# Wide tiles: input transposed by the DMA engines, and two outputs in seven block products

## The chip, the core and the metric

The kernel runs on one core of one Trainium2 chip. The core has five engines that run their own instruction streams and wait for each other through semaphores: TensorE (PE in the profile; its weight loads are PEld) for matrix products into PSUM, VectorE (DVE) and ScalarE (ACT) for elementwise work, GpSimd (POOL) for elementwise work and for issuing loads, and SyncE (SP), which issues the output's stores. Times are microseconds of the device for one execution; each kernel is run several times and the median is given.

## The reference

Eight batches of eight heads, 576 tokens, 64 elements a head: attention in a causal window of 64 tokens. Its result, 4608 tokens by 512, goes through a gated feed-forward layer of width 1536.

```python
def _attn_ref(q, k, v):
    B, H, S, D = q.shape
    window = 64
    scale = 1.0 / np.sqrt(D)
    scores = scale * np.matmul(q, k.transpose(0, 1, 3, 2))
    pos = np.arange(S)
    rel = pos[:, None] - pos[None, :]
    mask = (rel >= 0) & (rel < window)
    scores = np.where(mask, scores, -1000000000.0)
    scores = scores - np.max(scores, axis=-1, keepdims=True)
    attn = np.exp(scores)
    attn = attn / (np.sum(attn, axis=-1, keepdims=True) + 1e-09)
    return np.matmul(attn, v).astype(np.float32)

def _moe_ref(x, w_gate, w_val, w_out):
    gate = np.maximum(x @ w_gate, 0.0)
    val = x @ w_val
    return (gate * val @ w_out).astype(np.float32)
```

Inputs and output are 32-bit floats in HBM; the kernel multiplies in 16-bit floats and sums in 32.

## The kernel before

The 4608 tokens are cut into ten tiles: tiles 0 to 3 of 384 tokens and the wide tiles 4 to 9 of 512 (`starts`, `widths`, lines 70 to 76). The text counts them from 0, so the eighth and ninth tile are 7 and 8, and `LAST` is 9. Only the wide tiles matter here.

**Attention of a wide tile.** Queries are handled in quads of four windows of 64 (`q_st`, `scores`): TensorE makes the scores of four head pairs in four PSUM banks (line 253), ScalarE takes the exponential into `pw` (line 389), VectorE masks it (line 394). `values(t, hh)` then makes the product with v for one half of the heads (`t_pv`, line 422) into three banks, with the sum of the weights as a 65th column; VectorE takes the reciprocal (`t_recip`, line 436), multiplies (`t_norm`, line 441) into the tile `xw`, and transposes in blocks of 32x32 (`t_turn`, line 447) into `xt`, where channels lie on partitions. Before the change the rows of a result are channel groups: 32 tokens of each of four heads lie on the 128 partitions.

**Hidden stage (`fast_hidden`).** The gate is a plain product (line 582) that ScalarE passes through a relu into `r` (line 586). The product with `w_val` uses Strassen's scheme in Winograd's form: seven block products P1 to P7 (line 573) in place of eight. It needs four differences of the input's blocks (`x_form`, tile `xc`, line 459, on VectorE) and four of the weight's blocks (`w_form`, tile `vs`, line 480, on GpSimd). Partial sums are combined on the way: bank A collects P1, P6, P7, P4; ScalarE copies it out between them (`snap`, line 593), VectorE adds such a copy to bank B or C (`add`, tile `vsum`, line 600), and GpSimd multiplies by the relu into `g_sb` (line 606); one quarter is multiplied by VectorE straight from PSUM (`direct`, line 613). P3 goes into bank C after the sum with "u3" has been read from it. This is done in three groups of four chunks of 128 hidden channels. A pair such as (1,1) names the half of the hidden channels and the half of the tokens of a product in `g_sb`.

**Output stage (`fast_output`).** For each of four blocks of 128 tokens, 12 products of 512 columns with `wo` (line 658) go into one bank; ScalarE copies it (line 663) into one of three `o_sb` buffers and SP stores it (line 665). Ahead of the four blocks stand, for the tiles to come, the two halves of `values(t + 1)` and two `scores(t + 2)` (list `between`). The last block of tile 9 is cut in three (`output_last`, line 703).

**What sets the order.** Nothing reorders instructions on the chip. The `Weaver` (lines 20 to 43) writes the order out when the kernel is built: it keeps a planned clock, which the issue of a product moves on, and a heap of callbacks with due times; `W.advance` issues what is due. `bank()` and the loops on `done` issue callbacks ahead of time where a product needs their result or a bank. Each engine then runs its stream in this order, and an instruction that waits holds up what stands behind it on its engine. GpSimd's stream has also the loads of q, k (line 173) and v (line 199), the copies that spread v over partitions (lines 208, 210), and SP's stream the stores. A tile pool gives each tile name some buffers (`bufs`); a new use waits for the old one's readers.

`zero` and `zero32` (lines 732 to 735) are tiles of zeros for a few products early on that keep TensorE busy.

Of the kernel before, what the change touches and what calls it, by code (L numbers as in the profile page):

```python
# [10 lines left out]
FP32 = mybir.dt.float32  # L11
# [35 lines left out]
def kernel(  # L47
# [25 lines left out]
    NL = (NT - NS * TT) // WT  # L73
    assert NT == NS * TT + NL * WT and TT % 128 == 0
# [20 lines left out]
    vs = persist.tile([128, 4, 2, 128 * HF], FP16)  # L95
    qTs = [persist.tile([128, 2, S, 2], FP16, name=f"qT{i}") for i in range(2)]
# [307 lines left out]
    def t_pv(t, hh, banks, give):  # L404

        if t not in wides:
            wides[t] = {"pv": {}, "give": give, "x": a_n.tile([128, 2, WS, 2, D // 2], FP16, name="xw", bufs=1),
                        "r": a_n.tile([128, 2, WS, 1], FP32, name="rw")}
        d = wides[t]
        d["pv"][hh] = banks  # L410
        unread.update(map(id, banks))
        for qh in range(2):
            qd = 2 * (t - NS) + qh
            while quads[qd].get("masked", 0) < G:
                W.pop()
            for i in range(QW):
                b, vw = divmod(q_window(qd, i), NG)
                for s in range(2):
                    n = 2 * (QW * qh + i) + s
                    to = banks[n // BS][:, VW * (n % BS):]  # L420
                    for j in range(G):
                        nc.tensor.matmul(to[32 * j:32 * j + 32, 0:D + 1],  # L422
                                         quads[qd]["p"][j][:, QW * hh + i, 32 * s:32 * s + 32],
                                         v16s[b % 2][:, vw, G * hh + j, 0:D + 1],
                                         start=True, stop=True, skip_group_check=True)

    def t_part(d, hh, k):

        s0, s1 = BS * k, min(BS * k + BS, WS)
        return d["pv"][hh][k][:, 0:(s1 - s0) * VW].rearrange("p (s c) -> p s c", c=VW), s0, s1  # L430

    def t_recip(t, hh):
        d = wides[t]
        for k in (2, 0, 1):
            pv, s0, s1 = t_part(d, hh, k)
            nc.vector.reciprocal(d["r"][:, hh, s0:s1], pv[:, :, D:D + 1])

    def t_norm(t, hh, k):
        d = wides[t]
        pv, s0, s1 = t_part(d, hh, k)  # L440
        nc.vector.tensor_tensor(d["x"][:, hh, s0:s1], pv[:, :, 0:D].rearrange("p s (c e) -> p s e c", e=2),
                                d["r"][:, hh, s0:s1, :, None].to_broadcast([128, s1 - s0, 2, D // 2]), MUL)
        read(d["pv"][hh][k], d["give"])

    def t_turn(t, hh):
        dst = xt_tile(t)[:, 2 * hh:2 * hh + 2].rearrange("p e (s c) -> p s e c", c=32)
        nc.vector.transpose(dst, wides[t]["x"][:, hh])
# [4 lines left out]
    def x_form(t, n):  # L452
# [3 lines left out]
        xt, xc = xt_tile(t), xcs[t]  # L456
        b11, b12, b21, b22 = (xt[:, 2 * k:2 * k + 2, HT * h:HT * h + HT] for k in range(2) for h in range(2))
# [5 lines left out]
    def values(t, hh, T, banks=None):  # L463
# [7 lines left out]
        for n in ((0,), (1, 2, 3))[hh]:  # L471
            W.at(T + 4.0 + 0.4 * n, lambda n=n: x_form(t, n))

    def w_form(n, j):
# [5 lines left out]
        nc.gpsimd.tensor_tensor(vs[:, n, :, c], x, y, op)  # L480

# [65 lines left out]
    def fast_hidden(t):  # L547

        g_sb, done = gs[t] = g_sb_p.tile([128, NF, WT], FP16, name="g_sb"), {}
        xt, xc = xt_tile(t), xcs[t]  # L550
        b11, b12, b21, b22 = (xt[:, 2 * k:2 * k + 2, HT * h:HT * h + HT] for k in range(2) for h in range(2))
# [3 lines left out]
        def group(j):  # L555
# [21 lines left out]
            def gate(n):  # L577
# [3 lines left out]
                for k in range(NC):  # L581
                    nc.tensor.matmul(to, wg[:, k, 128 * ff:128 * ff + 128], xt[:, k], start=(k == 0), stop=(k == NC - 1))  # L582
                W.clock += 4 * (WT + 7) / 2400.0

                def relu():
                    nc.scalar.activation(r4[:, n], to, ACT.Relu)  # L586
                    free.append(to)
# [8 lines left out]
            def add(delay, to, name, last, n, h):  # L596

                def summed():
# [5 lines left out]

                    def mult():
                        nc.gpsimd.tensor_tensor(gh[:, 2 * j + HF * n:2 * j + HF * n + 2, h], rh[:, 2 * n:2 * n + 2, h], pair(v), MUL)  # L606
                        done[2 * j + HF * n, h] = done[2 * j + HF * n + 1, h] = True
                    W.at(max(W.clock, at["relus", n]) + 0.7, mult)
# [30 lines left out]
            add(0.1, "C", "u2", True, 0, 1)  # L639

        for j in range(NF // 4):
            group(j)

    F_LAST = [f for j in range(NF // 4) for f in (2 * j + HF, 2 * j + HF + 1, 2 * j, 2 * j + 1)]

    def fast_output(t, between):

        g_sb, done = gs[t]
        for sub, before in enumerate(between):
# [11 lines left out]
            def evac(op=op, sub=sub):  # L661
# [3 lines left out]
                nc.sync.dma_start(out[bass.ds(starts[t] + sub * 128, 128)], o_sb)  # L665
            W.at(W.clock, evac)

# [28 lines left out]
    def output_last(t):  # L696
# [3 lines left out]
        for c0, c1, queue in ((0, 256, nc.sync), (256, 384, nc.sync), (384, DM, nc.scalar)):  # L700
# [4 lines left out]
            o_sb = consts.tile([128, c1 - c0], FP32, name=f"o_last{c0}")  # L705
            nc.scalar.copy(o_sb, op[:, 0:c1 - c0])
            queue.dma_start(out[bass.ds(starts[t] + last * 128, 128), c0:c1], o_sb)
# [11 lines left out]
    with tc.manual_schedule():  # L719
# [12 lines left out]
        zero = consts.tile([128, 512], FP16)  # L732
        nc.vector.memset(zero, 0.0)
        zero32 = consts.tile([128, 384], FP32)
# [89 lines left out]
        for u in (4, 5):  # L824
            W.at(52.0, lambda u=u: v_spread(u, pool))
        pair(2, 55.5, 58.5, 61.9)
# [22 lines left out]
        LAST = NS + NL - 1  # L849
        SLOTS = (2.6, 6.53 + 0.8, 6.53 + 2.6, 2 * 6.53 + 0.8)  # L850

        def ahead(t):
# [9 lines left out]
            if t == NS - 1:  # L862
                qk_ahead(NS + 1, T + 11.5, (0.0, 1.4, 8.0, 9.4))
                for qd, x in ((0, 6.0), (1, 9.2), (2, 22.6), (3, 25.8)):
# [34 lines left out]
        for t in range(NS, NS + NL):  # L899
# [10 lines left out]
            if t == LAST:  # L910
                fast_output(t, between[:-1])
                W.drain()
                output_last(t)
            else:
# [32 lines left out]
```

## Time and profile before

| | |
|---|---|
| time, median of 3 runs | 321.8 us (321.8 to 322.2) |
| the profiled execution: its time, its span | 322.06 us, 320.2 us |
| granted clock of TensorE | 0.995 |
| start of the wide tiles' hidden stages, 4 to 9 | 122.3, 157.2, 190.2, 223.1, 256.0, 287.4 us |
| last product | 317.4 us |

The span is the stretch between the first and the last instruction that the profile shows; the rest of the time lies around it. Busy shares are averages over stages, so the stages are looked at one by one: a window gives the busy time of each engine between two times, the timeline gives instructions in order, and the chain of waits goes back from the last instruction to what released each step.

### The profile page before, as it was taken

The numbers are of one execution on the slowest core, as the hardware profiler recorded it, in microseconds if no ns is written. First come the engines' busy times: TensorE is split into PE (matmuls) and PEld (weight loads), VectorE is DVE, ScalarE is ACT, GpSimd is POOL, SyncE is SP. The second block draws the span as 40 slices with busy tenths as digits, with TensorE's granted clock in tenths as the row PEclk, the third lists the DMA queues.
The fourth block names the chain that finished last, engine by engine and source line by source line (L and its number), as shares of the span: only waits on it lengthen the run. The fifth ranks groups of instructions, "written<-read, shape, count | busy, mean of one in ns | idle before, by whom it ended". The sixth has DMA issues, their size and how long they took to land.

```text
span 320.2 us, 9481 instructions
## 1 busy us (share of the span) xinstructions
PE 308.8 (96%) x4077; PEld 190.1 (59%) x4077; DVE 203.2 (63%) x397; ACT 158.1 (49%) x310; POOL 177.8 (56%) x206
## 2 busy tenths in 40 slices
PE   4799999999899999999999999999999999999996
PEld 2586958655546555665566556655665566546654
DVE  6937962667993996779576857686337734643420
ACT  3644325533524616752765276627652666326632
POOL 8859336215988506799168925980495036404540
PEclk9889999999999999999999999999999999999999
DMA  8999998946299149806910691039001100020002
GB/s 218 183 196 205 194 120 161 171 98 99 30 174 165 21 90 160 57 1 104 219 36 0 97 220 43 2 50 127 35 0 34 69 34 3 2 98 35 0 33 102
DMA packets 52491, 29.52 MB, mean 92 GB/s; under 512 B 38880, under 2 KB 43872, under 8 KB 52448
## 3 DMA queue, kind: packets, MB, share of 16 engines
q0 software_dynamic: 46688, 18.29, 49.3%
q1 hardware_dynamic: 5616, 10.55, 9.3%
q8 instruction: 32, 0.52, 0.7%
q14 instruction: 11, 0.09, 0.1%
q10 hardware_dynamic: 144, 0.07, 0.1%
HBM read 37.75 MB, written 9.44 MB: 147 GB/s over the span
## 4 chain that ended last, share of the span: by engine, by line
PE 89%; DVE 3%; ACT 2%; POOL 2%; DMA 2%; issue 1%; DVEq 0%; POOLq 0%
PE bank L658 19%; PE bank L582 19%; PE bank L538 17%; PE bank L573 17%; PE bank L673 10%; PE bank L253 3%; PE bank L422 2%; DVE p L292 2%; DMA v<-in_v_dram 2%; ACT pw L389 1%; PE bank L311 1%; DVE g_sb L525 1%; PE bank L703 1%; POOL v L199 1%; DVE qT L193 0%
## 5 line engine op out<-in xcount | busy, mean ns | idle before, releaser
L606 POOL TENSOR_TENSOR g_sb<-r,vsum 128x512 f16<-128x512 f32 x54 | 68.1, 1276 | 77.7 <-DVE vsum L600 75.7
L600 DVE TENSOR_TENSOR vsum<-bank,snap 128x512 f32<-128x512 f32 x54 | 37.3, 691 | 60.1 <-PE bank L573 36.5
L582 PE MATMUL bank<-xt,wg 128*128 128x512 f16 x288 | 73.9, 379 | 0.0
L658 PE MATMUL bank<-wo,g_sb 128*128 128x512 f16 x276 | 62.9, 380 | 0.0
L586 ACT ACTIVATE r<-bank 128x512 f32<-128x512 f32 x72 | 43.2, 600 | 32.3 <-PE bank L582 32.3
L658 PEld LDWEIGHTS <-g_sb 128*128 128x128 f16 x276 | 25.5, 98 | 28.9
L582 PEld LDWEIGHTS <-wg 128*128 128x128 f16 x288 | 28.2, 98 | 18.6
L525 DVE TENSOR_TENSOR g_sb<-r,bank 128x384 f16<-128x384 f32 x48 | 25.9, 550 | 20.3 <-PE bank L538 18.8
L522 ACT ACTIVATE r<-bank 128x384 f32<-128x384 f32 x48 | 23.7, 496 | 29.4 <-PE bank L538 20.3
L573 PEld LDWEIGHTS <-vs 128*128 128x128 f16 x288 | 28.0, 98 | 15.6 <-issue 1.6
L538 PE MATMUL bank<-xt,wg 128*128 128x192 f16 (+1 forms) x256 | 36.5, 296 | 0.5 <-DVE g_sb L525 0.4
L663 ACT COPY o_sb<-bank 128x512 f32<-128x512 f32 x23 | 13.5, 586 | 45.2 <-PE bank L658 43.2
L593 ACT COPY snap<-bank 128x512 f32<-128x512 f32 x54 | 31.6, 586 | 8.4 <-PE bank L573 8.4
L199 POOL DMA_DIRECT2D v<-in_v_dram x41 | 34.7, 865 | 1.8 <-DMA q<-in_q_dram 1.0
L538 PE MATMUL bank<-xt,wv 128*128 128x192 f16 (+1 forms) x256 | 34.3, 286 | 0.0
L673 PE MATMUL bank<-wo,g_sb 128*128 128x512 f16 x144 | 32.8, 379 | 0.2 <-DVE g_sb L525 0.2
L538 PEld LDWEIGHTS <-wg 128*128 128x128 f16 x256 | 24.3, 102 | 9.8 <-issue 0.9
L573 PE MATMUL bank<-xc,vs 128*128 128x256 f16 x216 | 29.4, 272 | 0.4 <-ACT snap L593 0.4
L208 POOL COPY v<-v 64x512 f16<-64x512 f16 (+1 forms) x22 | 16.1, 732 | 23.7 <-DMA v<-in_v_dram 22.6
L538 PEld LDWEIGHTS <-wv 128*128 128x128 f16 x256 | 22.9, 98 | 8.1
L394 DVE TENSOR_TENSOR pw<-pw,mask 128x512 f16<-128x512 f16 x48 | 20.2, 437 | 11.2 <-ACT pw L389 10.5
L389 ACT ACTIVATE pw<-bank 128x512 f16<-128x512 f32 x48 | 25.9, 608 | 1.5 <-PE bank L253 1.0
(69 smaller groups left out, 358.6 us busy)
## 6 DMA issues: line engine op xcount, KB each, us to landing
out_dram<-o_sb SPq DMA_DIRECT2D x35, 256.0 KB, 3.0
k<-in_k_dram POOLq DMA_DIRECT2D x15, 288.0 KB, 5.3
q<-in_q_dram POOLq DMA_DIRECT2D x15, 288.0 KB, 7.3
v<-in_v_dram POOLq DMA_DIRECT2D x31, 128.0 KB, 8.0
wg<-in_moe_w_gate_dram POOLq DMA_DIRECT2D x6, 256.0 KB, 6.4
wv<-in_moe_w_val_dram POOLq DMA_DIRECT2D x6, 256.0 KB, 8.2
wo<-in_moe_w_out_dram POOLq DMA_DIRECT2D x3, 512.0 KB, 11.9
v<-in_v_dram POOLq DMA_DIRECT2D x10, 64.0 KB, 5.9
```

The costliest lines, as they stand in the source:

```text
L199: nc.gpsimd.dma_start(v16s[b % 2][lo:hi, g, :, 0:64], v[b, :, 64 * g - 64 + lo:64 * g - 64 + hi].rearrange("h p d -> p h d"))
L389: nc.scalar.activation(d["p"][g].rearrange("p n c -> p (n c)"), d["st"][g], ACT.Exp, scale=scale)
L525: nc.vector.tensor_tensor(g_sb[:, f:f + w, c0:c0 + n], part(r_sb), part(h2), MUL)
L538: nc.tensor.matmul(h[:, b * n:b * n + n], wt[:, c, (f + b) * 128:(f + b) * 128 + 128], xt[:, c, c0:c0 + n], start=(c == 0), stop=(c == NC ...
L573: nc.tensor.matmul(at[to][:, HT * i:HT * i + HT], w[:, k, 128 * i:128 * i + 128], x[:, k], start=(first and i == 0 and k == 0), stop=(k == ...
L582: nc.tensor.matmul(to, wg[:, k, 128 * ff:128 * ff + 128], xt[:, k], start=(k == 0), stop=(k == NC - 1))
L586: nc.scalar.activation(r4[:, n], to, ACT.Relu)
L593: nc.scalar.copy(at[name], at["A"])
L600: nc.vector.tensor_tensor(v, at[to], at[name], ADD)
L606: nc.gpsimd.tensor_tensor(gh[:, 2 * j + HF * n:2 * j + HF * n + 2, h], rh[:, 2 * n:2 * n + 2, h], pair(v), MUL)
L658: nc.tensor.matmul(op, g_sb[:, f, 128 * sub:128 * sub + 128], wo[:, f], start=(i == 0), stop=(i == NF - 1))
L673: nc.tensor.matmul(op, g_sb[:, f, bass.ds(sub * 128, 128)], wo[:, f], start=(f == 0), stop=(f == NF - 1))
```

## The change

It has four parts.

- `t_pv` takes halves of the tokens (quads) in place of halves of the heads, and puts 128 tokens on the partitions, even ones ahead of odd ones. `t_norm` writes `xw` so that a row is a token. `t_turn` is now a DMA that transposes, issued by SP, in place of the VectorE transpose. The order of tokens within `xt` changes, so the views in `x_form`, `fast_hidden` and the stores (`rows_of`) change with it: the two halves of the tokens are the even and the odd ones. All four `x_form` stand behind the second half, 2 us later on the planned clock than before.
- `wo_form`: twelve differences of `wo`'s blocks on GpSimd into a new tile `ws`; six are planned at 50.5 and later, six in tile 3.
- For tiles 7 and 8 `g_form` makes twelve differences of `g_sb`'s blocks on VectorE into `s_sb`, and `block_output` makes the output by seven block products in place of eight, with three copies by ScalarE into `snap`, three sums by VectorE and one copy by ScalarE into `o_sb`, and four stores. In the last group of these tiles one product (`late`) moves from GpSimd to VectorE.
- Memory: the zeros lie in `ws`, `o_last` becomes `o_sb`, `s_sb` takes a buffer of `g_sb`.

```diff
+    ws = persist.tile([128, 4, HF, DM // 2], FP16)
...
-        for qh in range(2):
-            qd = 2 * (t - NS) + qh
-            while quads[qd].get("masked", 0) < G:
-                W.pop()
-            for i in range(QW):
-                b, vw = divmod(q_window(qd, i), NG)
-                for s in range(2):
-                    n = 2 * (QW * qh + i) + s
-                    to = banks[n // BS][:, VW * (n % BS):]
-                    for j in range(G):
-                        nc.tensor.matmul(to[32 * j:32 * j + 32, 0:D + 1],
-                                         quads[qd]["p"][j][:, QW * hh + i, 32 * s:32 * s + 32],
-                                         v16s[b % 2][:, vw, G * hh + j, 0:D + 1],
-                                         start=True, stop=True, skip_group_check=True)
+        qd = 2 * (t - NS) + half
+        while quads[qd].get("masked", 0) < G:
+            W.pop()
+        for n in range(WS):
+            blk, h = divmod(n, H)
+            to = banks[n // BS][:, VW * (n % BS):]
+            for s in range(2):
+                for w in range(2):
+                    i = 2 * blk + w
+                    b, vw = divmod(q_window(qd, i), NG)
+                    nc.tensor.matmul(to[64 * s + 32 * w:64 * s + 32 * w + 32, 0:D + 1],
+                                     quads[qd]["p"][h % G][:, QW * (h // G) + i, s:64:2],
+                                     v16s[b % 2][:, vw, h, 0:D + 1],
+                                     start=True, stop=True, skip_group_check=True)
...
-    def t_turn(t, hh):
-        dst = xt_tile(t)[:, 2 * hh:2 * hh + 2].rearrange("p e (s c) -> p s e c", c=32)
-        nc.vector.transpose(dst, wides[t]["x"][:, hh])
+    def t_turn(t, half):
+        nc.sync.dma_start(xt_tile(t).rearrange("p c n -> p (c n)")[:, 2 * WT * half:2 * WT * half + 2 * WT].rearrange("p (g n) -> p g n", n=128),
+                          wides[t]["x"][half].rearrange("p e s c -> p (e s c)"), transpose=True)
...
-        for n in ((0,), (1, 2, 3))[hh]:
-            W.at(T + 4.0 + 0.4 * n, lambda n=n: x_form(t, n))
+        for n in ((), range(4))[hh]:
+            W.at(T + 6.0 + 0.4 * n, lambda n=n: x_form(t, n))
...
+    def wo_form(n, j):
+
+        f1, f2 = slice(HF + 2 * j, HF + 2 * j + 2), slice(2 * j, 2 * j + 2)
+        c1, c2 = slice(0, DM // 2), slice(DM // 2, DM)
+        b11, b12, b21, b22 = wo[:, f1, c1], wo[:, f1, c2], wo[:, f2, c1], wo[:, f2, c2]
+        to = ws[:, :, 2 * j:2 * j + 2]
+        x, y = ((b12, b11), (b22, to[:, 0]), (b22, b12), (b21, to[:, 1]))[n]
+        nc.gpsimd.tensor_tensor(to[:, n], x, y, SUB)
...
+    def g_form(t, n, j, eng):
...
+        f1, f2 = slice(HF + 2 * j, HF + 2 * j + 2), slice(2 * j, 2 * j + 2)
+        h1, h2 = slice(HT, WT), slice(0, HT)
+        a11, a12, a21, a22 = g_sb[:, f1, h1], g_sb[:, f2, h1], g_sb[:, f1, h2], g_sb[:, f2, h2]
+        for f, h in (((f1, 0), (f2, 0)), ((f1, 1),), ((f1, 0), (f1, 1)), ((f2, 1),))[n]:
+            while (f.start, h) not in done:
+                W.pop()
...
+        x, y, op = ((a21, a22, ADD), (to[:, 0], a11, SUB), (a11, a21, SUB), (a12, to[:, 1], SUB))[n]
+        eng.tensor_tensor(to[:, n], x, y, op)
...
+                    late = blocks_out(t) and j == NF // 4 - 1 and (n, h) == (0, 0)
...
-                        nc.gpsimd.tensor_tensor(gh[:, 2 * j + HF * n:2 * j + HF * n + 2, h], rh[:, 2 * n:2 * n + 2, h], pair(v), MUL)
+                        (nc.vector if late else nc.gpsimd).tensor_tensor(gh[:, 2 * j + HF * n:2 * j + HF * n + 2, h], rh[:, 2 * n:2 * n + 2, h], pair(v), MUL)
...
+            if blocks_out(t):
+                late = j == NF // 4 - 1
+                for n, x in ((2, 6.6), (0, 7.2), (1, 7.3), (3, 10.4)) if late else ((2, 9.9), (0, 10.0), (1, 10.1), (3, 10.9)):
+                    W.at(T + x, lambda n=n: g_form(t, n, j, nc.vector))
...
+    def block_output(t, after):
...
+        def product(name, to, first, subs=(0, 1)):
+            a, b, key = forms[name]
+            if first and to not in at:
+                at[to] = bank()
+            for fs in (range(0, HF - 2), range(HF - 2, HF)):
+                for i in subs:
+                    W.advance(W.clock)
+                    for f in fs:
...
+                        nc.tensor.matmul(at[to][:, HT * i:HT * i + HT], a[:, f, 128 * i:128 * i + 128], b[:, f],
+                                         start=(first and i == 0 and f == 0), stop=(f == HF - 1), skip_group_check=True)
+                        W.clock += (HT + 7) / 2400.0
...
+        run(0)
+        product("P1", "A", True)
+        snap("a1")
+        product("P5", "C", True)
+        run(1)
+        product("P6", "A", False)
+        snap("u2")
+        product("P2", "B", True, (0,))
+        run(2)
+        product("P7", "A", False)
+        snap("u3")
+        add(0.9, "C", "u3", False, 0, c2)
+        product("P2", "B", False, (1,))
+        add(0.1, "B", "a1", True, 1, c1)
+        product("P4", "A", False)
+        W.at(W.clock, direct)
+        run(3)
+        while ("summed", "u3") not in at:
+            W.pop()
+        product("P3", "C", False)
+        add(0.1, "C", "u2", True, 1, c2)
...
+        for j in range(NF // 4):
+            for n in range(2):
+                W.at(50.5 + 1.2 * (2 * j + n), lambda n=n, j=j: wo_form(n, j))
...
+                for j in range(NF // 4):
+                    for n in range(2, 4):
+                        W.at(T + 15.0 + 1.2 * (2 * j + n), lambda n=n, j=j: wo_form(n, j))
...
+            elif blocks_out(t):
+                block_output(t, between)
```

`run(i)` issues the attention work of the tiles to come, as `fast_output` does ahead of its block i; `add` and `direct` end with a store of one half of the tokens by one half of the columns.

## The prediction

> **What bounds the kernel now.** I read the busy table first, then the chain of waits, then single stretches of the timelines. The columns of the chain are start, length (both us), engine, tile, line, count.
>
> ```profile
> span 320.2 us, 9481 instructions
> ...
> PE 308.8 (96%) x4077; PEld 190.1 (59%) x4077; DVE 203.2 (63%) x397; ACT 158.1 (49%) x310; POOL 177.8 (56%) x206
> 223.10:256.00 32.90, 32.90 (x438) 19.59 (x437) 18.15 (x38) 18.49 (x33) 15.76 (x15) 1.00 0.09 33
> ...
> 275.56 0.62 PE bank L422 x56
> 276.18 2.70 PE bank L658 x12
> 278.88 0.62 PE bank L422 x60
> 279.50 7.88 PE bank L658 x36
> 287.38 0.44 PE bank L573 x4
> ...
> 290.48 0.87 PE bank L573 x8
> ...
> 306.98 7.77 PE bank L658 x36
> ```
>
> TensorE is the bound. In the third line (tile 7, in the columns PE, PEld, DVE, ACT, POOL, clock, DMA) it is busy for all 32.90 us at clock 1.00, while VectorE has 18.15 us of work. The chain stays on PE from 127 us to the end, so a matmul column saved there is time saved, and a wait put there is time lost. Each wide tile has a hidden stage (three groups), then an output stage with the next tile's attention values (L422) and scores (L253) between its products.
>
> **What the change removes on TensorE.** An output stage is 48 products of 512 columns: 7.77 / 36 = 0.216 us each, 10.36 us. In tiles 7 and 8 it becomes 7 x 2 x 6 = 84 products of 256 columns. The row for that shape is L573, 0.87 / 8 = 0.109 us: 9.14 us. The saving is 1.22 us a tile, 2.45 us in all. Attention values keep 128 small products a tile, but their weights are read with a step of two; L253 reads kT and q so, 64 products in 0.61 us against L422's 0.62, with one slow piece of 0.72 at 186.75. So 0 to 0.1 us a half, at most 1.2 in all; I take 0, as all but that piece stand at 0.61. The hidden stage's products read x in runs of 64 or 128 elements; by the same rows 0 to 0.1 / 64 us each, at most 0.8 us for the 288 of L582 and 216 of L573; I take 0. ScalarE writes r in such runs too (0.60, with idle time behind it): 0.
>
> **What it adds to VectorE and takes off.** Off: twelve transposes L447 of 1.24 us, 2.5 us a tile, which hid behind PE already. On, in each of tiles 7 and 8: twelve f16 differences of 128x512 (like L459, 0.42 us), three sums out of PSUM (like L600, 0.69), one product taken from GpSimd (both inputs in SBUF; between L613's 0.69 and GpSimd's own L606, 1.28; I take 0.69, the same engine): 5.0 + 2.1 + 0.7 = 7.8 us. VectorE's 18.15 - 2.5 + 7.8 = 23.5 us fits in 33 us; the order decides, not the sum. ScalarE trades four copies for three, 0.59 us each: nothing, as it is half idle.
>
> The differences meet a neighbour. Here are f16 operations of VectorE that run beside a two-input GpSimd operation (start, us):
>
> ```profile
> 148.28 1.29 DVE L459 TENSOR_TENSOR xc<-xt 128x512 f16<-128x512 f16 x1
> ...
> 147.96 1.30 POOL L606 TENSOR_TENSOR g_sb<-r,vsum 128x512 f16<-128x512 f32 x1
> ...
> 80.24 4.38 DVE L292 TENSOR_TENSOR p<-p,mask 128x384 f16<-128x384 f16 x4 [1.04 <-ACT p L287]
> ...
> 80.68 2.50 POOL L480 TENSOR_TENSOR vs<-wv 128x512 f16<-128x512 f16 x2
> ```
>
> The first takes 1.29 us instead of 0.42 and ends 0.3 us after GpSimd's 147.96 + 1.30; the four masks take 1.1 us each, one per GpSimd operation. So such an operation ends about 0.3 us after the GpSimd operation that it met. The PSUM-reading sums do not suffer (0.69 everywhere).
>
> *Tile 7.* In VectorE's new order the four differences of a group stand ahead of the next group's sum "C + u3" (before at 234.29 and 240.82), for which PE's product P3 waits (235.57, 242.09). GpSimd's three products of group 1 stand at 228.56, 231.67 and up to 234.17, its spreads between. The differences start at 232.6, and the last one needs the product that ends at 234.17: they are through at 235.2, the sum at 235.9, P3 0.4 us late. In the next group (GpSimd from 237.30 to 241.03) they end at 242.0 on the shifted clock, P3 another 0.3 late. Then, in the output stage: the first difference of group 3 waits for GpSimd's (1,1) product (done at 244.1, difference at 244.5), the sum follows (245.1) and the late product (245.75), P5's difference meets GpSimd's (0,1) product (245.2 to 246.5) and ends at 246.9, where PE stands since 246.1: 0.7 us; the scores wait 0.35 us for banks that VectorE normalizes later than before; P4 waits 0.3 us for a snapshot that stands behind three exponentials of 0.515. Sum: 0.7 + 1.35 = 2.05, less 0.3 us of pipeline drains that such waits absorb (12 products take 2.70 after a switch and 2.59 in a run, 0.11 each): 1.75 lost, 1.22 saved: 0.5 later. Without the neighbour's effect the same walk gives 0.7 lost: 0.5 earlier. Half of the differences wait for GpSimd's results anyway in either reading, so I take the middle: 0.
>
> *Tile 8.* There GpSimd has no spreads and is through with each group (265.29, 271.81) before the differences stand (265.4, 272.0): no wait in the hidden stage. In the output stage the same walk ((1,1) at 275.7, difference 276.1, sum 276.8, late product 277.4, P5's difference 278.55 behind GpSimd's (0,1), PE there since 278.3) gives 0.25 us at P5, 0.05 at P4 and P3 each: 1.22 - 0.35 = 0.9 saved; with the drain that is absorbed, 1.0.
>
> **GpSimd's twelve differences of wo** (like L480, 1.21 us) are all issued in order. Six stand among the copies after 45 us, ahead of four q/k loads and three v loads, which are issued up to 7 us later; the cover is GpSimd's idle 8.83 us before 62.05 and the loads' time in hand (k landed at 48.9 + 6.7 = 55.6, used from 66.65: 11 us). Without that cover it would cost the 7 us. Six stand behind tile 3's q loads: five from about 119.8 to 126.0, then five v loads (4.2 us), the sixth, then tile 4's first product, 1.8 us late (before: 129.67). GpSimd's later gaps (0.35 + 0.55) and the spreads absorb most; tile 4's output needs the last (0,0) product at 146.6 and gets it at 146.3. So 0, with 0.3 us to spare.
>
> **The moved transposes.** Each half (256 KB, SBUF to SBUF) is now a transfer on SP's queue, in order with the output stores. It waits for the norms; four x differences on VectorE and then PE's first product wait for its landing, and behind the x differences stand masks and the group's sums. So I take a margin for each tile, from the second half's issue (end of its norms) to PE's first product of the tile: tile 4: 117.8 to 122.3, 4.5 us for both halves at once; tile 5: 149.7 to 157.2, 7.5; tile 6: 182.6 to 190.2, 7.6; tile 7: 215.6 to 223.1, 7.5; tile 8, by the walk above: 250.7 to 256.4, 5.7; tile 9: 282.5 to 286.3, 3.8. Behind a waiting transfer on SP stand only stores whose copies come later (tile 4: transfer 146.4, first store 147.8), so its wait costs nothing; four stores a tile stay four, with rows of 1 KB instead of 2. No row shows such a transfer. The nearest are the stores (same queue and size), one alone, then issued at 147.8 and 151 beside a full load queue, and v loads with 1024 short packets:
>
> ```profile
> out_dram<-o_sb SPq DMA_DIRECT2D x8, 256.0 KB, 2.0
> ...
> out_dram<-o_sb SPq DMA_DIRECT2D x1, 256.0 KB, 8.7
> ...
> out_dram<-o_sb SPq DMA_DIRECT2D x1, 256.0 KB, 6.1
> ...
> v<-in_v_dram POOLq DMA_DIRECT2D x1, 128.0 KB, 9.3
> ```
>
> So 2.0 to 3.8 us quiet (3.8 is the shortest v load after 140 us), 6.1 to 9.3 us beside loads. I take the store, the nearer row: 2.0 quiet and 7.4 loaded, the mean of its two; every margin holds, tiles 5 and 6 barely. Price 0; bounds 0 and 6.2 (below).
>
> One page speaks against this move. The Trainium skill, "VectorE: DVE Perf Modes", section The three transpose paths, gives 1309 ns for a 128x128 block by DMA and 311 ns by VectorE; no run here shows the former. If the eight blocks of a half followed one another, 10.5 us by that figure (an estimate), all six margins would be missed, by some 26 us in all, and the kernel would take about 347 us.
>
> **Sum.** Tile 7: 0; tile 8: -1.0; all else 0. The profiled execution took 322.06 us (span 320.2 and 1.9 around it); it would take 321.1. The median of the runs is 321.8, 0.26 lower, so 320.8.
>
> **Rivals.**
> *All saved.* The neighbour's effect is smaller and PE never waits: -2.45, 319.4. For it: both tiles have idle VectorE time. Against it: the order above.
> *Given back in tile 7.* The effect holds fully (+0.5), tile 4's x differences, which run beside GpSimd's wo differences, cost 0.2: -0.3, 321.5, no change. For it: the 4.38 us row.
> *Late transposes: slower.* Place: starts of tiles 4, 5 and 6. At the v loads' pace, tile 4's two halves take 2 x 3.8 = 7.6 us against 4.9 from the first issue (2.7 late), tile 5 9.3 against 7.5 (1.8), tile 6 9.3 against 7.6 (1.7): 6.2 us, so 327; at half of that lateness 324, which I give as its time. It decides from 1.6 us of lateness in all. For it: a loaded queue at 146 to 161 and 179 to 192 us, stores that wait 3 us there for their first packet, and three o_sb buffers: the copy at 157.23 reuses the one whose store landed at 147.8 + 8.7 = 156.5. Against it: 7.5 us of margin, and a transfer that neither reads nor writes HBM.
> *The change does not act.* The 168 products would have to take 2.45 / 168 = 0.015 us more than L573's 0.109 to undo the saving; that row has the same shape in the same kernel, so I give this nothing.
>
> **How the numbers follow.** Forecast and its neighbour "all saved" (faster by over 0.2%, 0.64 us, about what a measurement of this kernel can tell from no change): 0.38 + 0.09 = 0.47. Given back: 0.17. Late transposes: 0.36. The likeliest case alone reaches from 319.9 (tile 7 also 0.5 earlier, tile 8 fully saved) to 321.5. The range runs from 319.4, all saved, to 325.5, between the slower rival's 324 and 327, leaving the worse half of it out.
>
> **What would show it.** Right: L740 (the block products) 84 per tile at 0.109; no wait of PE on xt's transfer at 122, 157, 190; P3 in tile 7 waiting some tenths for a sum; tile 8's output 1 us shorter than 11.8. Wrong: issue to landing of the transposes over 4 us in the quiet tiles or over 8 in tiles 5 and 6; PE idle at tile starts; VectorE's x differences waiting for DMA; o_sb copies waiting for landed stores.

## The result and the profile after

The changed kernel takes 350.9 us (median of 6 runs, 348.2 to 354.9), the kernel before 322.4 beside it: a ratio of 1.087, with a 95% interval from 1.082 to 1.092. It is slower by 28.5 us; the forecast was 320.8. Some executions are slower than the others of the same kernel, and the ratios and intervals of this text leave them out: here the one of 354.9 us, and with the idle products (under "The clock") those of 352.0 and 353.7 us, of which the second is the profiled one. The profiled execution took 352.5 us, with this page (the rows are the span, the busy time of the engines, the clock granted to TensorE in 40 slices, and the chain that ended last, by engine):

```profile
span 350.8 us, 9703 instructions
...
PE 314.4 (90%) x4149; PEld 197.7 (56%) x4149; DVE 208.3 (59%) x417; ACT 158.9 (45%) x310; POOL 190.5 (54%) x216
...
PEclk9999999999999978999789987999999999999999
...
PE 62%; DMA 19%; DVE 9%; POOL 6%; ACT 2%; issue 1%; DVEq 0%; ACTq 0%; POOLq 0%
```

PE is busy 5.6 us longer, though the block outputs should take 2.45 off, and for 90% of the span where it was 96%. DMA is in the chain, and the clock drops to 0.7 or 0.8 in three places. The chain of waits shows where (start, length, what):

```profile
119.92 10.16 DMA xt<-xw
...
158.09 14.18 DMA xt<-xw
172.27 0.14 issue
172.40 1.01 PE bank L611 x4
173.41 1.71 PE bank L620 x4
...
200.64 14.83 DMA xt<-xw
...
242.61 8.76 DMA xt<-xw
```

All four are DMA transposes, at the starts of tiles 4, 5, 6 and 7; at 156 us and later the chain before was PE alone. After the wait ahead of tile 5 four gate products take 1.71 us; undisturbed ones take 0.86. The timeline of PE gives what it stood still there, in brackets:

```profile
130.13 1.04 PE L611 MATMUL bank<-xt,wv 128*128 128x256 f16 x4 [6.88 <-DMA xt<-xw]
...
172.40 1.01 PE L611 MATMUL bank<-xt,wv 128*128 128x256 f16 x4 [6.74 <-DMA xt<-xw]
...
208.20 0.39 PE L255 MATMUL bank<-qT,kT 32*128 32x64 f16 x28 [3.04 <-issue]
...
215.52 1.04 PE L611 MATMUL bank<-xt,wv 128*128 128x256 f16 x4 [2.55 <-DMA xt<-xw]
...
251.50 0.60 PE L611 MATMUL bank<-xt,wv 128*128 128x256 f16 x4 [1.32 <-DMA xt<-xw]
```

The windows of both kernels from one tile's first hidden product to the next one's give the whole difference:

| stretch | before, us | after, us | difference |
|---|---|---|---|
| span's start to tile 4 | 122.27 | 130.13 | +7.86 |
| tile 4 | 34.72 | 42.27 | +7.55 |
| tile 5 | 33.02 | 43.12 | +10.10 |
| tile 6 | 32.91 | 35.98 | +3.07 |
| tile 7 (block output) | 32.87 | 34.74 | +1.87 |
| tile 8 (block output) | 31.42 | 31.17 | -0.25 |
| tile 9 to the span's end | 33.04 | 33.41 | +0.37 |

So 28.6 of 30.6 us lie at and between the late tiles. PE's waits for xt are 6.88 + 6.74 + 2.55 + 1.32 = 17.5 us and its stop in the scores at 205 us is 3.0. Some 7.6 us are slower products after such waits (hidden stages: tile 4 1.5, tile 5 2.6, tile 6 1.6; output of tile 5: 1.9), by the lengths of these stages less their waits (the output of tile 5 behind the stop, at a granted clock of 0.75 from 208.5 to 215.5 us). The two block outputs together cost 1.6 us where they should have saved 1.0. The transposes' times from issue to landing stand in the list of DMA issues for stretches of the trace (tile 5's second half, tile 6's second, tile 8's pair):

```profile
xt<-xw SPq DMA_TRANSPOSE x1, 14.2
...
xt<-xw SPq DMA_TRANSPOSE x1, 14.8
...
xt<-xw SPq DMA_TRANSPOSE x2, 3.1
```

Quiet, a transpose takes 3.1 us; beside loads, 13.7 to 14.8 in tiles 5 and 6, and 5.2 to 10.2 in tiles 4 and 7.

### The profile page after: what moved, and what is told of

It reads as the page before. It is cut to its first block, busy times and chain, and to the rows that moved or that the text cites. A ratio compares the mean times of both kernels' runs of the same rounds, so it can differ in the third digit from the quotient of the medians.

```text
span 350.8 us, 9703 instructions
## 1 busy us (share of the span) xinstructions
PE 314.4 (90%) x4149; PEld 197.7 (56%) x4149; DVE 208.3 (59%) x417; ACT 158.9 (45%) x310; POOL 190.5 (54%) x216
## 4 chain that ended last, share of the span: by engine, by line
PE 62%; DMA 19%; DVE 9%; POOL 6%; ACT 2%; issue 1%; DVEq 0%; ACTq 0%; POOLq 0%
PE bank L620 16%; PE bank L611 14%; DMA xt<-xw 14%; PE bank L574 12%; PE bank L800 6%; PE bank L705 6%; PE bank L740 4%; DMA wv<-in_moe_w_val_dram 3%; DMA wg<-in_moe_w_gate_dram 2%; DVE s_sb L515 2%; POOL g_sb L646 2%; DVE p L294 2%; PE bank L424 2%; PE bank L255 2%; DVE xw L443 1%
## 5 line engine op out<-in xcount | busy, mean ns | idle before, releaser
L646 POOL TENSOR_TENSOR g_sb<-r,vsum 128x512 f16<-128x512 f32 x52 | 66.5, 1293 | 105.0 <-DVE vsum L638 103.2
L620 PE MATMUL bank<-xt,wg 128*128 128x512 f16 x288 | 77.2, 392 | 0.0
L705 PE MATMUL bank<-wo,g_sb 128*128 128x512 f16 x180 | 42.8, 391 | 0.0
L611 PE MATMUL bank<-xt,wv 128*128 128x256 f16 x144 | 23.3, 288 | 17.5 <-DMA xt<-xw 17.5
L574 PE MATMUL bank<-xt,wg 128*128 128x192 f16 (+1 forms) x256 | 35.2, 286 | 2.0 <-DVE xt L354 0.9
L611 PEld LDWEIGHTS <-wv 128*128 128x128 f16 x216 | 21.5, 101 | 26.4 <-DMA xt<-xw 10.4
L800 PE MATMUL bank<-wo,g_sb 128*128 128x512 f16 x144 | 32.8, 379 | 0.2 <-DVE g_sb L561 0.2
L611 PE MATMUL bank<-xc,vs 128*128 128x256 f16 x216 | 30.7, 280 | 0.0
L705 PEld LDWEIGHTS <-g_sb 128*128 128x128 f16 x180 | 17.1, 100 | 20.0 <-issue 2.3
L396 DVE TENSOR_TENSOR pw<-pw,mask 128x512 f16<-128x512 f16 x48 | 19.9, 434 | 13.9 <-ACT pw L391 13.4
L462 DVE TENSOR_TENSOR xc<-xt 128x512 f16<-128x512 f16 x12 | 6.0, 500 | 37.3 <-DMA xt<-xw 37.3
```

Of the source, the lines that this page charges most:

```text
L574: nc.tensor.matmul(h[:, b * n:b * n + n], wt[:, c, (f + b) * 128:(f + b) * 128 + 128], xt[:, c, c0:c0 + n], start=(c == 0), stop=(c == NC ...
L611: nc.tensor.matmul(at[to][:, HT * i:HT * i + HT], w[:, k, 128 * i:128 * i + 128], x[:, k], start=(first and i == 0 and k == 0), stop=(k == ...
L620: nc.tensor.matmul(to, wg[:, k, 128 * ff:128 * ff + 128], xr[:, k // 2, k % 2], start=(k == 0), stop=(k == NC - 1))
L646: (nc.vector if late else nc.gpsimd).tensor_tensor(gh[:, 2 * j + HF * n:2 * j + HF * n + 2, h], rh[:, 2 * n:2 * n + 2, h], pair(v), MUL)
L705: nc.tensor.matmul(op, g_sb[:, f, 128 * sub:128 * sub + 128], wo[:, f], start=(i == 0), stop=(i == NF - 1))
L800: nc.tensor.matmul(op, g_sb[:, f, bass.ds(sub * 128, 128)], wo[:, f], start=(f == 0), stop=(f == NF - 1))
```

## The experiments

The theories: A, the transposes share the 16 DMA engines with the loads of q, k and v, in turns of one packet; B, a transpose is slow by itself; C, it is held up by the output stores in its own queue; D, TensorE's clock falls in a wait and makes the products behind it slow. For the block outputs: VectorE's order makes PE wait, or its meeting with GpSimd does.

### Each part alone

*The block outputs alone*: the kernel before with `wo_form`, `g_form`, `block_output`, VectorE transposes and the old order of tokens (the edit in part).

```diff
-        nc.sync.dma_start(xt_tile(t)..., transpose=True)
+        dst = xt_tile(t)[:, 2 * hh:2 * hh + 2].rearrange("p e (s c) -> p s e c", c=32)
+        nc.vector.transpose(dst, wides[t]["x"][:, hh])
```

> The kernel before with the block outputs of tiles 7 and 8 alone; VectorE transposes as before, so tile starts are free of the DMA transposes. If the forecast's walk holds (0 in tile 7, 1.0 saved in tile 8): about 1 us under before, 321.4 beside 322.4. If PE waits nowhere: 2.45 us under. If VectorE, which keeps its 2.5 us of transposes a tile and gets 7.8 more, is late in both tiles: 0 to 1.5 us over before. In the trace: tile 7's hidden and output stage 32.9 us before, 31.4 before in tile 8.

Measured: 333.2 us, 1.033 [1.030, 1.036]; no reading had this. Tile 7 took 36.2 us (+3.3), tile 8 32.8 (+1.3), and 4.8 us were lost in tile 4's output, where PE and GpSimd read (start, length):

```profile
123.88 1.15 POOL L491 TENSOR_TENSOR ws<-wo 128x512 f16<-128x512 f16 x1
...
130.15 4.26 POOL L201 DMA_DIRECT2D v<-in_v_dram  x5
134.38 1.21 POOL L491 TENSOR_TENSOR ws<-wo,ws 128x512 f16<-128x512 f16 x1
135.50 3.76 POOL L643 TENSOR_TENSOR g_sb<-r,vsum 128x512 f16<-128x512 f32 x3
```

```profile
150.65 0.60 PE L702 MATMUL bank<-wo,g_sb 128*128 128x512 f16 x2 [2.98 <-POOL g_sb L643]
```

Here the differences of wo stand behind q loads that wait for their buffers until 123 us; tile 4's first product on GpSimd starts at 135.5 instead of 129.67, and PE waits 2.98 us for the last one; the next twelve output products then take 4.45 us, where the later ones take 2.76. In the changed kernel these loads went out at 119.25 and 120.33 and the first difference ran at 120.92; PE stood there for xt anyway.

*The transposes alone*: the changed kernel with `blocks_out` false and without `wo_form`.

> The changed kernel without the block outputs and without the differences of wo: only the DMA transposes and their layout are left. If these make the loss alone (theory A, B or C): 349 to 352 us, PE waiting for xt at the starts of tiles 4 to 7. If the loss came from GpSimd's wo differences or the block outputs: under 330.

Measured: 347.3 us, 1.078 [1.073, 1.084]. The DMA transposes with their layout bring 25 us of the loss by themselves; PE waited for xt in tiles 4 to 7 and stopped for 2.97 us in the same scores.

### Why the transposes are late

*No loads.* From tile 3 on the q, k and v loads are left out and attention works on old data.

```diff
+        if late_loads[0] and b > 1:
+            nat[b, name, hh] = nat[b - 1, name, hh]
+            return
         tile_ = nat[b, name, hh] = a_in.tile(...)
...
+        if late_loads[0]:
+            return
         b, uu = divmod(u, UB)
```

> The changed kernel without the loads of q, k and v from tile 3 on; the attention of the wide tiles works on old data, the rest is the same. Theory A (the transposes share the DMA engines with these loads, packet by packet): the transposes land in 3 to 4 us everywhere, no wait at tile starts, 320 to 323 us. Theory B (a transpose of 256 KB is slow by itself): landing stays over 7 us in tiles 4 to 7, 345 us or more. Theory C (stores ahead in the same queue): landing falls little, 340 or more.

Measured: 326.6 us, 1.013 [1.010, 1.016], 3.6 over the range of A. Every transpose landed in 3.0 to 3.5 us:

```profile
DMA to landing us min/median/max: 3.0/3.1/3.5
```

PE waited for xt only 0.4 us, in tile 4. The stores stood in the queue as before, so C falls as a cause by itself, and B with it. Tiles 4 to 6 took 34.7, 32.9, 32.9 us, as before the change. What is left of the loss is not transposes: tile 7 again +1.95, and 2.7 us up to tile 4 (I put these down to VectorE's order, as kT's transposes no longer wait for loads; no run tried it).

*A plain copy in the transpose's place* (`transpose=True` and the blocked view left out):

> The changed kernel with a plain copy from xw to xt of the same 256 KB on the same queue at the same place, not transposed (the transposition is left out). If it is the transport beside the loads that is slow, whatever its kind: 13 to 15 us beside loads as the transposes, 345 to 351 us. If the 1024 short packets of the transposition are what loses against the loads: as the stores, 6 to 9 us loaded and 2 quiet; tile 4 late by 1 to 3 us, tiles 5 and 6 by 0 to 2, so 323 to 330 us.

Measured: 327.5 us, 1.016 [1.013, 1.020]. The copies landed in 2.2 to 8.6 us, in tile 6 in 7.8, where the transposes took 14.6 and 14.8. The same bytes on the same queue, beside the same loads, pass in about half the time. This copy moves 2048 B a packet, the transpose 256 B (1024 packets for 256 KB). The two differ in the transposing too; a transpose with longer packets was not run.

*Without q and k loads; without v loads*: one half each of the edit above.

> The changed kernel without the loads of q and k from tile 3 on (old data is used); v is loaded. If it is the q and k loads (packets of 2304 B, 1.15 MB a batch) that hold the transposes up: landing of 3 to 6 us. If it is the v loads with their short packets (128 B): landing stays at 10 to 14 us in tiles 5 and 6.

> The changed kernel without the loads of v from tile 3 on (old data is used); q and k are loaded. The reverse of the run before: landing of 3 to 6 us if the v loads hold the transposes up, 10 to 14 us in tiles 5 and 6 if q and k do. If both share by bytes: each of the two runs lies between, 5 to 10 us.

Measured (one execution each): 331.1 us without q and k, with landings of 3.1 and 9.2 in tile 5, 4.9 and 8.9 in tile 6; 342.2 us without v, with 11.7 to 13.9 there. Over all twelve transposes, first without q and k, then without v:

```profile
DMA to landing us min/median/max: 3.0/3.5/9.2
...
DMA to landing us min/median/max: 3.0/4.4/13.9
```

Both kinds of load hold the transposes up. Those of q and k cost more, but the v loads alone still triple a landing, more than the first expectation allowed (3 to 6 us), and PE waits 4.3 us for xt in that run.

The changed kernel's own packets say how. The list of queues (q0: the loads, q1: the transposes and stores; packets, MB, share of 16 engines' time) at 160 to 163 us beside q and k loads, at 169 to 171 beside v loads, and at 280 to 281 with no load:

```profile
q0 software_dynamic: 159, 0.33, 88.4%
q1 hardware_dynamic: 160, 0.04, 28.9%
...
q1 hardware_dynamic: 833, 0.21, 80.0%
q0 software_dynamic: 832, 0.10, 79.5%
...
q1 hardware_dynamic: 757, 0.19, 119.9%
```

159 and 160, 832 and 833: while both queues have work, one packet of the one goes for one packet of the other. Alone the transposes moved 757 packets in a us; beside q and k loads 53. In the packet records the median packet of q or k (2304 B) takes 0.191 us, one of v (128 B) or of a transpose (256 B) 0.031, one of a store (2048 B) 0.096. From the issue of tile 5's second half at 158.09 us to its landing at 172.27 all 2048 packets of both halves pass, with 359 of q and k, 2073 of v and 283 of stores. At these medians they fill the 16 engines for (2048 x 0.031 + 359 x 0.191 + 2073 x 0.031 + 283 x 0.096) / 16 = 14.0 us, and 14.2 were measured. This is an estimate: on average the packets take longer than these medians, and they overlap (the loads' share of 16 engines' time reached 112% from 157 to 158 us). The plain copy has 128 packets a half and needs that many fewer turns.

The turns do not explain everything. The first halves of tiles 5 and 6 stood 3.2 and 3.9 us before their first packet moved (1.2 when quiet). In tile 7, beside v loads alone, 1024 turns of 0.062 us over 16 engines would be 4.0 us, and the second half took 8.8, its packets starting 3.5 us after its issue, at 246.11; the store issued between the two halves landed at 246.22. What held the packets back in these places is open.

The Trainium skill, "DMA: Bandwidth & Descriptors", section Queues, rings and completion order, says this: each engine goes round the queues it has work for and takes a whole packet from one before it goes to the next. These counts agree, if a record of the trace is what the page calls a packet, which is not shown here.

### Loads moved

The loads of q, k and v for the wide tiles are issued away from the transposes; all is computed.

```diff
-                qk_ahead(NS + 2, T + 27.6, SLOTS)
-                v_ahead(NS + 1, T + 27.6)
+                qk_ahead(NS + 2, T + 27.6, SLOTS, [T + x for x in (13.5, 14.5, 28.8, 29.3)])
+                v_ahead(NS + 1, T + 27.6, 1.8)
...
-                    qk_ahead(t + 3, T + WIDE_T, SLOTS)
+                    qk_ahead(t + 3, T + WIDE_T, SLOTS, [T + x for x in (6.0, 10.0, 12.5, 17.0)])
...
-                    v_ahead(t + 2, T + WIDE_T)
+                    v_ahead(t + 2, T + WIDE_T, 1.5, 8.0)
```

The list gives the times of the four loads, the last two numbers the offsets of v's loads and of its spreads.

> The changed kernel with the loads of q, k and v for the wide tiles issued away from the transposes: q and k 4 to 15 us earlier, v 6 us later. Everything is computed. Theory A: transposes land in 3 to 6 us, PE waits little at the starts of tiles 4 to 7, 325 to 330 us (the 326.6 without loads, and up to 3 more for the loads that still meet a transpose or are late themselves). Without A: 345 or more.

Measured: 333.8 us, 1.034 [1.030, 1.037]: 17 us won, but the time is 4 us over the expected range. Landings had a median of 3.4 us and a longest of 8.0, and PE waited for xt only 0.5 us, in tile 7. What came in their place lies in tile 4, which took 42.3 us: its v loads stand between GpSimd's products now, and PE waits 5.0 us for g_sb and the second attention values with it.

*Moved again in tile 4, block output in tile 8 alone*: q's two loads and v's of tile 4 ahead of GpSimd's products (23.0 and -4.5 in place of 28.8, 29.3 and 1.8), wo's differences in tiles 6 and 7, and in tile 8 the second attention values ahead of P5 (the edit stands under "The block outputs").

> The changed kernel with the loads moved as in the run of that name, but in tile 4 ahead of GpSimd's products, which were held up there by the v loads behind them (5.0 us of waits); block output in tile 8 alone, wo's differences in tiles 6 and 7. Theory A: no wait at tile starts beyond some tenths, 322.5 to 325. If transposes still land late: PE waits for xt show it, 326 or more.

Measured: 338.7 us, 1.050 [1.047, 1.054]: a miss that shows A again. Without wo's differences ahead of them, the q loads went out at 118.1 and 119.2 and the v loads from 119.7, right on tile 4's two transposes (issued from 117.3 to 120.1), and the chain has:

```profile
118.79 10.93 DMA xt<-xw
```

PE waited 7.6 us for it, where the run before had no such wait (its q load there went out at 122.2, and the transposes landed in 3.4 and 3.1 us). Nor did the new order free tile 4's output: PE still waited 3.9 us for g_sb. The other tiles show the reverse; windows of tiles 6 and 7 of this run (columns: length, busy PE, PEld, DVE, ACT, POOL, then clock, DMA share, GB/s):

```profile
204.88:237.82 32.94, 32.94 (x437) 19.62 (x436) 22.79 (x46) 18.49 (x33) 25.98 (x25) 1.00 0.24 56
237.82:270.73 32.91, 32.91 (x438) 19.61 (x437) 16.69 (x38) 18.48 (x33) 23.54 (x23) 1.00 0.43 66
```

32.94 and 32.91 us, PE busy throughout at clock 1.00: DMA transposes with moved loads cost PE nothing in these tiles (32.91 and 32.87 before).

### The clock

24 products of 512 columns on any data, ahead of the first product of tiles 4, 5 and 6:

```diff
+            if j == 0 and t < NS + 3:
+                at["A"] = bank()
+                for _ in range(24):
+                    nc.tensor.matmul(at["A"], wo[:, 0, 0:128], wo[:, 1], start=True, stop=True, ...)
```

> The changed kernel with 24 idle products of 512 columns (5.2 us) ahead of the first product of tiles 4, 5 and 6, into a bank that is overwritten, so that TensorE does not stand while it waits for xt. Theory D (after a wait TensorE's granted clock is low for some us, which costs 1.5 us in tile 4, 2.6 in tile 5, 1.6 in tile 6 beyond the waits): about 5 us less than the changed kernel, 346, and the hidden stages of tiles 4 to 6 take 22.1, 20.3, 20.3 us instead of 22.8, 23.0, 21.9. If the longer hidden stages have another cause (VectorE's late x differences): 351, unchanged.

Measured: 351.0 us (median of 4 runs, 345.0 to 353.7), 1.078 [1.069, 1.088] beside 1.087 [1.082, 1.092]: as a time no difference from the changed kernel can be told. The stages can: in tile 5 the products covered the whole wait, in tiles 4 and 6 another 3.4 and 3.9 us of standing were left behind them. Tile 5's hidden stage in the changed kernel, then tiles 5's and 4's here:

```profile
172.40:195.36 22.96, 22.96 (x197) 14.30 (x197) 15.63 (x25) 12.22 (x21) 13.56 (x14) 0.88 0.28 34
```

```profile
174.19:194.48 20.29, 20.29 (x197) 13.43 (x197) 15.41 (x25) 12.11 (x21) 13.59 (x14) 1.00 0.31 35
132.19:155.96 23.77, 23.77 (x260) 14.81 (x261) 16.49 (x28) 15.46 (x28) 13.49 (x14) 0.88 0.31 21
```

The same 197 products in 20.29 us at clock 1.00 instead of 22.96 at 0.88, and 20.29 / 0.88 is 23.1: the lower clock is enough for the difference. In tile 6, where PE stood again, the stage stayed at 21.95. In tile 4 it grew: 23.77 us at 0.88, where the changed kernel had 22.82 at 0.93 and 22.1 were expected, though PE stood for 3.4 us in place of 6.9. So D is shown for tile 5, where the wait was covered in full; how far the clock falls after a shorter wait is open. The wait itself is not shortened by the products.

### The block outputs

*Tile 8 alone, with VectorE transposes.* wo's differences in tiles 6 and 7; the second attention values ahead of P5.

```diff
+        if t == LAST - 1:
+            run(1)
         product("P5", "C", True)
-        run(1)
+        if t < LAST - 1:
+            run(1)
```

> The kernel before with the block output in tile 8 alone; VectorE transposes everywhere, GpSimd's twelve differences of wo in tiles 6 and 7, where GpSimd has idle time, and the second half of tile 9's attention values ahead of P5. In the run with blocks alone, tile 8 took 1.35 us more than before, with PE waiting 1.84 us. If the differences of wo and the order were the cause of part of it: 0 to 0.5 us under before. If VectorE, which keeps its transposes, is what is late: 1 us over before.

Measured: 324.0 us, 1.0065 [1.0039, 1.0092], 2 us over before and so nearest to the reading that VectorE is late. Tile 8 took 32.99 us (+1.57).

*The same with DMA transposes for tiles 8 and 9.*

> The same with DMA transposes for tiles 8 and 9 alone, where no loads run and a transpose landed in 3.1 us; tiles 4 to 7 as before. In the changed kernel tile 8 took 0.25 us less than before, with waits of 0.3 us at P5, which the order now covers. Expected 0.3 to 0.7 us under before, about 321.6, which 5 rounds may just tell from no change; if the DMA transposes' latency or the wo differences cost elsewhere: same or 0.5 over.

Measured: 323.1 us, 1.0027 [1.0014, 1.0040]: slower by 0.3%, where faster was expected. Tile 8 took 32.12 us (+0.70). P5 no longer waits, but P3 does, for VectorE's sum of C and u3. PE, then VectorE:

```profile
286.76 1.47 PE L813 MATMUL bank<-wo,s_sb 128*128 128x256 f16 x12 [1.36 <-DVE o_sb L829]
```

```profile
285.68 0.43 DVE L526 TENSOR_TENSOR xc<-xt 128x512 f16<-128x512 f16 x1 [0.98 <-DMA xt<-xw]
286.02 0.68 DVE L829 TENSOR_TENSOR o_sb<-bank,snap 128x512 f32<-128x512 f32 x1
```

With the second attention values earlier, tile 9's x differences come ahead of this sum, and the first one waits for the transpose. With VectorE transposes (the run before) the same sum stood behind a transpose and three x differences and came at 286.65; P3 waited 2.24 us. So my order seems worse than that of the change. In the changed kernel's order tile 8 has no such wait and takes 31.2 us; that would put this run at about 322.2 (0.95 us less), no gain that can be measured, and it was not run.

*Both tiles, moved loads, the g_sb differences later, and wo's differences in tiles 5 and 6; in tile 8 the order of the two runs before:*

```diff
-                ... else ((2, 9.9), (0, 10.0), (1, 10.1), (3, 10.9)):
+                ... else ((2, 11.4), (0, 11.5), (1, 11.6), (3, 12.4)):
```

> As the run before, with block outputs in tiles 7 and 8, and in both the differences of g_sb of the first two groups planned 1.5 us later, behind the sum that P3 waits for. Theory order (VectorE's order makes P3 wait, 1.3 us in tile 7): those waits vanish, tile 7 takes 1 to 1.5 us less than the 34.8 of the changed kernel. Theory neighbour (an operation of VectorE's that meets GpSimd's ends late wherever it stands): P5's wait grows by as much as P3's falls, tile 7 stays at 34.5 or more.

Measured: 343.9 us, 1.068 [1.064, 1.072]; its tile 4 is as in the second run with moved loads (waits of 7.0 us for xt and 3.9 for g_sb). P3's waits in tile 7's hidden stage are gone (20.34 us instead of 21.91), and the wait is at P5:

```profile
262.33 0.78 PE L740 MATMUL bank<-ws,s_sb 128*128 128x256 f16 x4 [2.02 <-DVE s_sb L515]
```

Tile 7 took 35.6 us, 0.9 more than in the changed kernel. The order did make P3 wait, but the 1.3 us that this won came back at P5, whose wait grew by 1.1, as the theory of the neighbour had it: the work moved to where VectorE has attention values, sums and differences to do at once. Behind this wait the granted clock was 0.64 (262.3 to 267.1 us), and twelve products took 2.44 us instead of 1.49. Tile 8 took 33.8 us, 2.7 more than in the changed kernel, with waits of 1.0 us for a difference and 1.6 for the sum ahead of P3.

No version made here beats the kernel before.

## Why the prediction was wrong

*PE bounds the kernel; products saved are time saved.* Right, and for that reason waits at tile starts cost in full.

*Block products at 0.109 us.* Right: twelve in a row took 1.30 to 1.32 us in tile 8, from start to start. *PV with stepped weights, x in runs: 0.* Right: without loads the hidden stages took 20.34 us against 20.32.

*"Price 0; bounds 0 and 6.2".* This is the step that failed: the price of a transpose beside loads. The row was taken for its queue and its size, the stores with 7.4 us; the plain copy with the stores' packets took about that (5.9 to 8.6 beside loads), the transposes with eight times as many packets 13.7 to 14.8 in tiles 5 and 6. I had the v loads with their 1024 short packets as the upper bound, 9.3 us, which is about what a transpose takes beside v loads alone (8.9 and 9.2); but here it took turns with packets of q and k of 0.19 us each as well. I looked at how long a transfer is on the engines, not at how many turns it needs and what stands in between. "Every margin holds" was wrong by its own numbers too: tile 4's margin of 4.5 us is shorter than 7.4, with q loads planned right behind; its second half took 10.2 us there, and PE's longest wait, 6.88 us, followed. The rival *late transposes* had the place right, tiles 4, 5 and 6, with 3 to 6 us in all; the runs show 17.5 us of waits and 28.6 lost up to the start of tile 7.

*What a wait costs.* The sum counted it by its length. Behind such waits come 7.6 us of slower products; that the clock is the cause is shown by a run for tile 5.

*The margins* (4.5, 7.5 and 7.6 us) were read well: quiet transposes of 3.1 us meet every one of them but tile 4's, by 0.4 us. "Behind a waiting transfer on SP stand only stores whose copies come later" held too, though SP itself was busy for 6.3 and 7.9 us with issuing one transpose.

The Trainium skill's figure of 1309 ns a block ("VectorE: DVE Perf Modes", section The three transpose paths) led to an estimate of about 347 us, and 350.9 were measured; the closeness is luck. Eight blocks took 3.1 us when quiet, not 10.5, in tile 8 as in all tiles without loads.

*Tile 7: "I take the middle: 0".* Mis-sized. The walk with the neighbour's effect gave waits of 0.7 (P3), 0.7 (P5), 0.35 (scores), 0.3 (P4); measured were these (the scores did not wait):

```profile
265.28 0.60 PE L611 MATMUL bank<-xt,vs 128*128 128x256 f16 x4 [1.03 <-DVE vsum L638]
272.25 0.60 PE L611 MATMUL bank<-xt,vs 128*128 128x256 f16 x4 [0.28 <-DVE vsum L638]
276.68 0.61 PE L740 MATMUL bank<-ws,s_sb 128*128 128x256 f16 x4 [0.91 <-DVE s_sb L515]
282.90 1.47 PE L740 MATMUL bank<-ws,g_sb 128*128 128x256 f16 x12 [0.23 <-ACT snap L750]
```

2.45 us, with +1.87 for the tile. PE was also busy for 32.28 us, 0.63 more than the 32.87 before less the 1.22 saved; the runs do not show with what. The neighbour's effect was there, and an average with a reading that left it out had no ground: VectorE's differences beside GpSimd's products (first line: two of them, 0.42 us each alone)

```profile
261.09 2.04 DVE L515 TENSOR_TENSOR s_sb<-g_sb 128x512 f16<-128x512 f16 x2
...
275.25 1.37 DVE L515 TENSOR_TENSOR s_sb<-g_sb 128x512 f16<-128x512 f16 x1
```

*Tile 8: -1.0.* Mis-sized, -0.25 measured. P5 waited 0.30 us (0.25 expected). P7, P4 and P3 each start 0.11 to 0.19 us late behind the copy of bank A or the sum; 0.05 each had been put on two of them. The last 0.2 us I put down to pipeline drains at these stops.

*GpSimd's differences of wo: 0.* Nearly so in this order: 0.46 us at 45 us (below), and no wait in tile 4 without loads. It was not robust: in the run with blocks alone the same twelve cost about 4.8 us.

*VectorE is relieved by 2.5 us of transposes.* True, and worth more than I said: with VectorE transposes the block outputs lost 3.3 and 1.3 us, with DMA transposes 1.9 and -0.25.

## What to carry to other kernels

Price a transfer that shares the DMA engines by its number of packets and by the packets of the other queues that it will alternate with, not by its bytes alone: a transpose of 256 KB in 256 B packets went from 3 to 14 us beside loads of 2304 B and 128 B packets, to 9 beside the 128 B ones alone, and took 3.2 to 7.1 in tiles 5 and 6 and 3.1 to 3.3 in tile 7 once the loads were issued at another time. A margin that a quiet transfer meets is no margin if loads are planned into it, and here 20.5 us of standing on TensorE were followed by 7.6 us in slower products. Before an operation is moved onto an engine whose idle time is enough in sum, look at the few us in which its results are needed: moving it later only moved the wait.

## What the runs showed of the hardware

- A VectorE copy from SBUF to SBUF is held as well as a two-input operation. At 43 us in the changed kernel, beside GpSimd's differences of wo, the copies that spread v took 1.26 and 1.13 us; in the kernel before 0.42 and 0.29. They ended 0.3 and 0.2 us after the two differences (42.65 to 43.90 and 43.98 to 45.19 us), and PE waited 0.46 us for the second.

```profile
42.92 1.26 DVE L210 COPY v<-v 64x1024 f16<-64x1024 f16 x1
44.22 1.13 DVE L212 COPY v<-v 64x512 f16<-64x512 f16 x1
```

- SP needs 1.23 us to issue a quiet transpose and 0.47 for the plain copy of the same size; beside loads up to 7.9.
- PE stopped for 3.04 us in the middle of 64 score products at 205 us, waiting for nothing that the profile shows, and in the same place for 2.97 us with the transposes alone and 1.80 without v loads. One packet of the instruction queue (16 KB) falls into that stretch. Without q and k loads, without any loads, and with the idle products the stop was gone. That instructions too waited for the DMA engines is only argued from this.
- Not tried: the stores on another queue. In the run without loads they stayed where they were and the transposes landed in 3.1 us; what another queue would win beside loads is open.
